# Weight additions and lower parts on VectorE, products with V in one run, and a planner with other durations: an attention and SoLU kernel on one core

## The chip, the cores and the metric

The kernel runs on one core of a Trainium2 chip. Its engines are TensorE (PE in the profile), VectorE (DVE), ScalarE (ACT), GpSimd (POOL) and SyncE (SP), which here only issues transfers. Each engine takes its instructions in the order in which the program has them. The metric is the device time of one execution in microseconds, lower being better.

## The reference

Causal attention by blocks of 64, for 8 batches of 8 heads with 576 tokens and 64 columns a head; then two projections with a SoLU and a normalisation between them, on 4608 tokens:

```
scores = scale * q @ k.T                       # masked to block_i >= block_j
attn   = softmax(scores)
x      = (attn @ v), heads side by side        # 4608 x 512
h      = x @ w_in                              # 512 x 1024
solu   = h * softmax(h)
ln     = (solu - mean) / sqrt(var + 1e-6) * g_ln
out    = ln @ w_out                            # 1024 x 512
```

The weights come as float64, q, k and v as float32.

## The kernel before

The work falls into three kinds, which are all described to a planner as operations with an engine, a duration, what they read and write, and a key.

- **Weights** (`prep`, lines 316 to 337): 16 chunks of 128x512 words of float64. A chunk is loaded into `ub` (two buffers), limited on DVE (L323), scaled (L326 on DVE, or L324 on ACT), shifted (L327) and given its sign (L328) on DVE; POOL adds the lower word as an integer (L329); chunks of `w_out` are scaled by `g_ln` (L331, L332). Then it is split into an exact pair: an upper part (L333 on ACT or L334 on DVE) and the lower part, the difference of the two (L335, on POOL). The intermediate values lie in `xt[2]` and `ob`.
- **Attention** (`attention`, lines 374 to 546), for 32 pairs of heads, four pairs to a batch. Queries and keys are loaded and transposed (L400); but for the first four pairs, they are split into upper and lower parts (L416 to L430). Scores are made in six groups of PSUM columns (L441, L445, L449), masked (L465), the maxima taken on DVE (L469), the exponentials on ACT (L473), the sums inverted on DVE (L480, L481), and the probabilities scaled on POOL (L488) or DVE (L489). TensorE transposes them (L499), ACT copies them out (L371), and TensorE multiplies them with V (L533): two heads side by side, each with 64 columns of the array, in float32. There are two such operations for a pair, one for the first 256 queries (`ph` 0, four products) and one for the rest (`ph` 1, ten products); each opens a single-bank PSUM tile of its own when it comes up. Results are copied to `xt` (three batches deep).
- **Projections** (`moe`, lines 549 to 643), for 36 tiles of 128 tokens: `x` is split (L564, L568), multiplied with `w_in` in two halves of 12 products (L589), then on DVE and ACT the maximum, the exponentials into `ub`, and the product with the sum (L595 to L598); POOL centres (L599), ACT squares (L601), POOL takes the root (L612, L613), TensorE transposes (L624), ACT and DVE split (L628, L629), TensorE multiplies with `w_out` (L637), and the result is scaled (L641) and stored (L643).

The order on every engine is worked out when the program is built, by `Schedule.run` (lines 97 to 171): a list schedule over the dependences. Whenever an engine is free, it takes, of the operations that are ready, the one with the smallest key that finds its PSUM tile free (two tiles of two banks, "D", and four of one bank, "S"). Keys come from `PARAMS`, one offset for each kind of operation, plus the number of the pair or of the tile. An operation may have alternatives on other engines, each with a penalty that is added to its key; an alternative whose penalty is 3 or more is not offered (L69). `START` and `LAT` hold the engines' first free times and the delays between engines. The instructions are then emitted in that order. On the chip, semaphores enforce the dependences; the planned times themselves enforce nothing.

Of the kernel before, what the change touches and what calls it, by code (L numbers as in the profile page):

```python
# [11 lines left out]
F32 = mybir.dt.float32  # L12
# [19 lines left out]
NPT = 2  # L32
START = {"PE": 0.0, "ACT": 2930.0, "DVE": 0.0, "POOL": 2500.0, "SP": 560.0}
PARAMS = {
# [6 lines left out]
    "a_sp32": -5.767, "a_lf": -3.555, "a_w": 15.208, "a_xh": 37.196, "a_xl": 48.757, "a_c": 6.341,  # L41
    "a_o": 13.796, "ns32": 4, "np": 32, "l0": -6.655, "a_cl": 5.076,
# [7 lines left out]
class Schedule:  # L50
    """Orders the operations of all engines: a list schedule over their dependences, with
    durations from shapes alone. PSUM slots (of one or two banks) are given out as it goes,
    and an operation that several engines can do goes to the one that is free for it first."""
# [43 lines left out]
    def run(self):  # L97
# [5 lines left out]
        engfree = {e: START[e] for e in engs}  # L103
        events = [(t, i, 0, None, None) for i, t in enumerate(sorted(START.values()))]
# [12 lines left out]
        while events:  # L117
            t = events[0][0]
            while events and events[0][0] <= t:
                _, _, kind, o, e = heapq.heappop(events)  # L120
                if kind == 1:
# [566 lines left out]
```

## Time and profile before

| what | value |
|---|---|
| timed runs | 816.08 us median of 3 (815.44 to 816.29) |
| span of the profiled execution | 814.3 us (no other time of that execution is given) |
| TensorE busy | 787.6 us, 97% |
| DVE, ACT, POOL busy | 60%, 68%, 38% |
| mean granted TensorE clock | 0.994 |

The span runs from the first to the last instruction. The timed runs hold 1.8 us more than the span at the median. A matmul's end is modelled, so where the exact cost of a group of matmuls matters, the step from its start to the start of what follows is the better measure. "L533" is line 533 of the kernel.

### The profile page before, as it was taken

Reading aid. Unit: us, or ns where it says so; the run is one execution under the profiler, and the core shown is the slowest. Engines: PE = TensorE matmul, PEld = TensorE weight load, DVE = VectorE, ACT = ScalarE, POOL = GpSimd, SP = SyncE. Lnnn points to the kernel's source line nnn. Section 1 sums busy time; section 2 is a strip of 40 time slices with the busy share of each in tenths; the row PEclk is TensorE's granted clock in tenths of the full one; section 3 lists DMA queues with packets and bytes.
Section 4 is the critical chain, followed back from the end, with each engine's and each line's share of the span. In section 5 each row is a group of like instructions: output and inputs, shape, how many; then the busy total and the mean of one; then the engine's idle time right before and its main releaser. Section 6 shows DMA issues by size and latency. Waiting matters only on the chain.

```text
span 814.3 us, 14121 instructions
## 1 busy us (share of the span) xinstructions
PE 787.6 (97%) x4711; PEld 635.9 (78%) x4711; DVE 492.3 (60%) x1200; ACT 557.0 (68%) x1441; POOL 308.6 (38%) x468
## 2 busy tenths in 40 slices
PE   6878899999999999999999999999999999999998
PEld 5545678888888888888888888888888888788886
DVE  5999986655665555566665555555666655333332
ACT  6778787686877777777787777777777777434332
POOL 3567772243443323333333323233333333132210
PEclk9999999999999999999999999999999999999999
DMA  7457534143443343333333333433343320000000
GB/s 210 117 146 181 140 83 105 49 102 82 109 101 92 88 101 101 93 95 96 94 90 79 83 94 87 101 101 96 92 101 88 95 63 29 14 27 26 14 27 39
DMA packets 132760, 71.84 MB, mean 88 GB/s; under 512 B 118864, under 2 KB 118864, under 8 KB 132688
## 3 DMA queue, kind: packets, MB, share of 16 engines
q1 hardware_dynamic: 131632, 70.68, 34.0%
q8 instruction: 37, 0.61, 0.3%
q10 hardware_dynamic: 1056, 0.26, 0.2%
q14 instruction: 35, 0.29, 0.1%
HBM read 36.70 MB, written 9.44 MB: 57 GB/s over the span
## 4 chain that ended last, share of the span: by engine, by line
PE 86%; DVE 9%; issue 2%; ACT 1%; POOL 1%; DMA 0%; SPq 0%; DVEq 0%; POOLq 0%
PE ps L637 24%; PE ps L589 23%; PE ps L533 10%; PE ps L499 9%; PE ps L449 8%; PE ps L624 5%; PE ps L400 3%; PE ps L445 3%; DVE nm L469 2%; DVE pb L489 1%; DVE xt L326 1%; DVE xt L328 1%; DVE xt L327 1%; PE ps L441 1%; DVE ks L420 1%
## 5 line engine op out<-in xcount | busy, mean ns | idle before, releaser
L488 POOL TENSOR_SCALAR pb<-pb,rz 128x512 f32<-128x512 f32 (+4 forms) x270 | 148.8, 571 | 179.0 <-DVE rz L481 164.1
L473 ACT ACTIVATE pb<-ps,nm 128x128 f32<-128x128 f32 (+4 forms) x288 | 155.7, 551 | 61.6 <-DVE nm L469 61.5
L469 DVE TENSOR_REDUCE nm<-ps 128x1 f32<-128x128 f32 (+4 forms) x288 | 133.0, 504 | 4.3 <-PE ps L445 1.2
L599 POOL TENSOR_SCALAR ub<-ub,ms 128x1024 f32<-128x1024 f32 x36 | 41.0, 1140 | 190.0 <-DVE ms L598 190.0
L499 PE MATMUL ps<-ident,pb 128*128 128x128 f32 x800 | 106.0, 275 | 7.1 <-ACT pb L473 3.3
L371 ACT ACTIVATE pt<-ps 128x512 f32<-128x512 f32 (+1 forms) x224 | 108.7, 553 | 4.9 <-PE ps L499 4.3
L499 PEld LDWEIGHTS ps<-ident,pb 128*128 128x128 f32 x800 | 92.6, 141 | 23.3 <-ACT pb L473 3.6
L533 PE MATMUL ps<-pt,vr 128*64 128x320 f32 (+4 forms) x896 | 101.3, 366 | 0.7 <-ACT pt L371 0.5
L533 PEld LDWEIGHTS ps<-pt,vr 128*64 128x64 f32 x896 | 58.8, 137 | 41.7 <-issue 5.5
L449 PE MATMUL ps<-ks,qs 128*128 128x384 f32 (+1 forms) x448 | 84.5, 328 | 1.7 <-DMA qs<-qs 1.2
L589 PE MATMUL ps<-wih,xh 128*128 128x512 f32 x288 | 82.2, 407 | 2.9 <-DVE qtl L428 2.9
L637 PE MATMUL ps<-woh,ch 128*128 128x512 f32 x288 | 83.6, 411 | 0.0
L629 DVE TENSOR_TENSOR cl<-ps,ch 128x512 fp32r<-128x512 f32 x72 | 49.3, 685 | 56.6 <-ACT ch L628 56.6
L589 PE MATMUL ps<-wil,xh 128*128 128x512 f32 x288 | 79.6, 399 | 0.0
L637 PE MATMUL ps<-wol,ch 128*128 128x512 f32 x288 | 79.0, 396 | 0.0
L637 PE MATMUL ps<-woh,cl 128*128 128x512 f32 x288 | 78.8, 395 | 0.0
L589 PE MATMUL ps<-wih,xl 128*128 128x512 f32 x288 | 78.2, 393 | 0.0
L449 PEld LDWEIGHTS ps<-ks,qs 128*128 128x128 f32 x448 | 68.6, 191 | 7.2 <-ACT xh L564 1.0
L641 ACT ACTIVATE ob<-ps,ms 128x512 f32<-128x512 f32 x36 | 24.7, 687 | 71.5 <-PE ps L637 66.6
L596 ACT ACTIVATE ub<-ps,ms 128x1024 f32<-128x1024 f32 x36 | 40.1, 1115 | 46.2 <-DVE ms L595 46.1
L589 PEld LDWEIGHTS ps<-wil,xh 128*128 128x128 f32 x288 | 54.9, 191 | 12.9
L637 PEld LDWEIGHTS ps<-woh,cl 128*128 128x128 f32 x288 | 54.1, 188 | 13.0
(79 smaller groups left out, 1238.6 us busy)
## 6 DMA issues: line engine op xcount, KB each, us to landing
qs<-qs SPq DMA_DIRECT2D x56, 288.0 KB, 4.1
out_dram<-ob SPq DMA_DIRECT2D x36, 256.0 KB, 2.0
qr<-in_q_dram SPq DMA_DIRECT2D x64, 128.0 KB, 3.0
vr<-in_v_dram SPq DMA_DIRECT2D x64, 128.0 KB, 2.5
ks<-k2h SPq DMA_DIRECT2D x56, 144.0 KB, 2.5
kr<-in_k_dram SPq DMA_DIRECT2D x62, 128.0 KB, 2.7
ub<-in_moe_w_in_dram SPq DMA_DIRECT2D x8, 512.0 KB, 3.6
ub<-in_moe_w_out_dram SPq DMA_DIRECT2D x8, 512.0 KB, 3.7
```

Of the source, the lines that this page charges most:

```text
L371: op("ACT", t_act(n_), lambda: ACT.activation(aps()[0], aps()[1], AF.Copy, scale=scale), r=r, w=w, key=key, ps=ps, alts=[("DVE", t_dve(n_) ...
L449: PE.matmul(t[:, off : off + wid[u]], qs[h][:, 640 * n_ + 128 * i_ : 640 * n_ + 128 * i_ + 128], ks[h][:, 0 : wid[u]], start=n_ == 0, stop ...
L469: op("DVE", t_dve(wid[u]), lambda sp=sp, off=off, u=u: DVE.tensor_reduce(out=nm_[u], in_=PS(sp)[:, off : off + wid[u]], axis=AX.X, op=ALU. ...
L473: op("ACT", t_act(wid[u], 186), lambda sp=sp, off=off, u=u, zg=zg, zc=zc: ACT.activation(pb[:, poff[u] : poff[u] + wid[u]], PS(sp)[:, off ...
L488: op("POOL", 0.836 * nn + 243, lambda b=b, nn=nn, zg=zg, zc=zc: POOL.tensor_scalar(out=pb[:, poff[b] : poff[b] + nn], in0=pb[:, poff[b] : ...
L499: PE.transpose(t[:, (s_ - c0) * P : (s_ - c0 + 1) * P], pb[:, poff[b] + j * P : poff[b] + (j + 1) * P], ident)
L533: PE.matmul(PS(av)[half[h], 64 * o_ : 64 * (o_ + n_)], vt[:, j, 64 * h : 64 * h + 64], pt_.rearrange("p s q -> p (s q)")[:, 128 * s_ + 64 ...
L589: PE.matmul(o_, a_[:, c, :], w_[:, c, s_], start=(si == 0 and c == 0), stop=(si == 2 and c == NKI - 1))
L599: op("POOL", 1097, lambda: POOL.tensor_scalar(out=u, in0=u, scalar1=m[:, 3:4], scalar2=1.0, op0=ALU.add, op1=ALU.mult), r=[uk, ("m3", i)], ...
L624: PE.transpose(t_[:, c * P : (c + 1) * P], u[:, (4 * hf + c) * P : (4 * hf + c + 1) * P], ident)
L629: op("DVE", t_dve(512), lambda cs=cs, cps=cps: DVE.tensor_tensor(out=cl[:, cs, :].rearrange("p c q -> p (c q)"), in0=PS(cps), in1=ch[:, cs ...
L637: PE.matmul(o_, a_[:, c, :], w_[:, c, :], start=(hf == 0 and si == 0 and c == 0), stop=(hf == 1 and si == 2 and c == 7))
```

## The change

It has four parts. The integer addition of the weights and their lower part become DVE operations of 602 ns each, with POOL as the alternative. The two operations that multiply with V become one, which opens both PSUM tiles at once. The planner gets other durations for products and float32 products, adds 130 ns where TensorE changes between products with V and all else (`mode`), and plans POOL's operations, and those DVE operations that are marked `port`, never at the same time. All keys, penalties and offsets in `PARAMS` are new.

```diff
+SWITCH = 130.0
-    "nd": 2, "ld": 50.439, "lv": 1.808, "q": -3.52, "qe": 1.142, "s": 6.097, "se": -34.711, "sr": -9.155,
-    "sp": -24.637, "pt": -53.902, "pe": -29.441, "av": -40.478, "ae": -54.031, "x": -19.096, "h0": 30.197,
-    "hs": 1.049, "h": 10.087, "he": 5.197, "c": 29.273, "sq": 24.027, "ct": -50.339, "ce": -26.902,
-    "o": 12.508, "oe": 52.668, "w0": 4.753, "w1": 3.56, "q32": -49.338, "qe32": 2.512, "s32": -30.884,
-    "se32": -21.58, "sr32": -9.773, "sp32": 10.661, "pt32": -1.589, "pe32": 9.069, "av32": -26.682,
-    "ae32": -42.402, "ld32": 8.508, "lv32": 16.251, "e0": 19.063, "e1": 23.219, "e2": 43.479, "a_sp": 40.963,
-    "a_sp32": -5.767, "a_lf": -3.555, "a_w": 15.208, "a_xh": 37.196, "a_xl": 48.757, "a_c": 6.341,
-    "a_o": 13.796, "ns32": 4, "np": 32, "l0": -6.655, "a_cl": 5.076,
+    "nd": 2, "ld": 51.667, "lv": -25.298, "q": 16.851, "qe": 21.577, "s": -46.724, "se": -35.56,
+    "sr": -64.883, "sp": 19.339, "pt": -9.35, "pe": -19.617, "av": -20.093, "ae": -61.172, "x": -18.296,
+    "h0": 5.994, "hs": 0.904, "h": 12.384, "he": -10.186, "c": 23.52, "sq": 33.665, "ct": -55.927,
+    "ce": -21.489, "o": 14.183, "oe": 21.926, "w0": 13.58, "w1": 5.806, "q32": -88.948, "qe32": 7.175,
+    "s32": -11.147, "se32": -18.711, "sr32": -21.226, "sp32": -7.207, "pt32": 34.929, "pe32": 32.662,
+    "av32": -29.049, "ae32": -107.21, "ld32": 4.757, "lv32": 133.636, "e0": 4.803, "e1": 13.081,
+    "e2": 16.285, "a_sp": 21.679, "a_sp32": -3.355, "a_lf": -4.456, "a_w": 9.152, "a_xh": 36.812,
+    "a_xl": 79.986, "a_c": -9.941, "a_o": -99.362, "ns32": 4, "np": 32, "l0": -17.25, "a_cl": 33.492,
+    "a_ai": 9.64,
...
-    def op(self, eng, dur, fn, r=(), w=(), key=0.0, opens=None, ps=None, tail=0.0, alts=()):
+    def op(self, eng, dur, fn, r=(), w=(), key=0.0, opens=None, ps=None, tail=0.0, alts=(), port=False, mode=0):
+        o.port, o.mode = port, mode
-        o.uses = ps if ps is not None else opens
+        o.opens = () if opens is None else opens if isinstance(opens, tuple) else (opens,)
+        o.uses = o.opens if ps is None else (ps,)
-        if o.uses is not None:
-            self.users[o.uses] = self.users.get(o.uses, 0) + 1
-            (w if eng == "PE" else r).append(("ps", o.uses))
+        for x in o.uses:
+            self.users[x] = self.users.get(x, 0) + 1
+            (w if eng == "PE" else r).append(("ps", x))
...
+        portfree, mode = 0.0, 0
...
-                    if o.uses is not None:
-                        left[o.uses] -= 1
-                        if left[o.uses] == 0:
-                            heapq.heappush(events, (t + LAT[o.eng]["PE"], n, 3, o, None))
+                    for x in o.uses:
+                        left[x] -= 1
+                        if left[x] == 0:
+                            heapq.heappush(events, (t + LAT[o.eng]["PE"], n, 3, x, None))
-                    free[self.kind[o.uses]].append(self.slot[o.uses])
+                    free[self.kind[o]].append(self.slot[o])
-                    if o.opens is not None:
-                        if not free[self.kind[o.opens]]:
+                    port = e == "POOL" or e == "DVE" and o.port
+                    if port and portfree > t:
+                        heapq.heappush(events, (portfree, n, 0, None, None))
+                        n += 1
+                        continue
+                    if o.opens:
+                        kinds = [self.kind[x] for x in o.opens]
+                        if any(len(free[k]) < kinds.count(k) for k in kinds):
-                    elif o.uses is not None:
-                        until = max([v for x, v in held[o.uses].items() if x != e], default=0.0)
+                    elif o.uses:
+                        until = max([v for x, v in held[o.uses[0]].items() if x != e], default=0.0)
...
-                if best.opens is not None:
-                    self.slot[best.opens] = free[self.kind[best.opens]].pop(0)
-                    held[best.opens] = {}
-                if best.uses is not None:
-                    held[best.uses][e] = t + best.dur + 128
+                if e == "PE" and best.mode != mode:
+                    best.dur += SWITCH
+                    mode = best.mode
+                if e == "POOL" or e == "DVE" and best.port:
+                    portfree = t + best.dur
+                for x in best.opens:
+                    self.slot[x] = free[self.kind[x]].pop(0)
+                    held[x] = {}
+                for x in best.uses:
+                    held[x][e] = t + best.dur + 128
...
-        return max(107.0, n / 2.4 + 2.5)
+        return max(109.0, 0.4453 * n + 3.5)
-        return max(224.0, n / 0.6 + 29) if fp32 else max(106.0, n / 2.4 + 53.0)
+        return max(214.0, n / 0.6) if fp32 else max(106.0, n / 2.4 + 53.0)
...
-        op("POOL", 1225, lambda: POOL.tensor_tensor(out=T1.bitcast(I32), in0=T1.bitcast(I32), in1=T3.bitcast(I32), op=ALU.add), r=[k1, k3], w=[k1], key=key)
...
+        op("DVE", 602, lambda: DVE.tensor_tensor(out=T1.bitcast(I32), in0=T1.bitcast(I32), in1=T3.bitcast(I32), op=ALU.add), r=[k1, k3], w=[k1], key=key, port=True,
+           alts=[("POOL", 1225, lambda: POOL.tensor_tensor(out=T1.bitcast(I32), in0=T1.bitcast(I32), in1=T3.bitcast(I32), op=ALU.add), K["a_ai"])])
...
-        op("POOL", 1225, lambda: POOL.tensor_tensor(out=lo, in0=T1, in1=hi.bitcast(F32), op=ALU.subtract), r=[k1, (name, "h")], w=[(name, "l")], key=key,
-           alts=[("DVE", 602, lambda: DVE.tensor_tensor(out=lo, in0=T1, in1=hi.bitcast(F32), op=ALU.subtract), K["a_w"])])
...
+        op("DVE", 602, lambda: DVE.tensor_tensor(out=lo, in0=T1, in1=hi.bitcast(F32), op=ALU.subtract), r=[k1, (name, "h")], w=[(name, "l")], key=key, port=True,
+           alts=[("POOL", 1225, lambda: POOL.tensor_tensor(out=lo, in0=T1, in1=hi.bitcast(F32), op=ALU.subtract), K["a_w"])])
...
-            av = newps("S")
-            js = range(5) if ph else range(2)
-            def avmm(av=av, js=js, ph=ph):
+        avs = [newps("S"), newps("S")]
+        def avmm():
+            for ph, js in ((0, range(2)), (1, range(5))):
-                            PS(av)[half[h], 64 * o_ : 64 * (o_ + n_)],
+                            PS(avs[ph])[half[h], 64 * o_ : 64 * (o_ + n_)],
-            sel = [c for c in ptc if (c[1] <= 6) == (ph == 0)]
-            ptk = [(x, p % NPT, c0) for x in ("pt", "pt2") for c0, _ in sel]
-            op("PE", 54 + sum(t_two(64 * mov(j, 0, ph)[2], True) for j in js), avmm, r=ptk + [f"vr{i}"], key=kk, opens=av)
+        ptk = [(x, p % NPT, c0) for x in ("pt", "pt2") for c0, _ in ptc]
+        op("PE", sum(t_two(64 * mov(j, 0, ph)[2], True) for ph, js in ((0, range(2)), (1, range(5))) for j in js), avmm, r=ptk + [f"vr{i}"], key=kk, opens=tuple(avs), mode=1)
...
+            av = avs[ph]
...
-            op("PE", 12 * 216, hmm, r=wk + [("xh", i), ("xl", i)], key=key + K["h"], opens=hps if hf == 0 else None, ps=hps)
+            op("PE", 12 * 231.5, hmm, r=wk + [("xh", i), ("xl", i)], key=key + K["h"], opens=hps if hf == 0 else None, ps=hps)
...
-            op("PE", 12 * 216, omm, r=wk + [("ch", hf), ("cl", hf), ("ch2", hf)], key=key + K["o"], opens=ops_ if hf == 0 else None, ps=ops_)
+            op("PE", 12 * 231.5, omm, r=wk + [("ch", hf), ("cl", hf), ("ch2", hf)], key=key + K["o"], opens=ops_ if hf == 0 else None, ps=ops_)
```

Lines that differ only by `port=True` are left out: the mark goes on L323, L326, L327, L328, the two alternatives L332 and L334, the scaling of probabilities (L488, L489), the splitting of `x` (L564, L568, and their DVE forms) and the centring (L599, L600). Penalties of 3 or more still keep an alternative out: with the new values that holds for POOL's integer addition (`a_ai`) and lower part (`a_w`), not for DVE's centring (`a_c`) and scaling of the output (`a_o`).

More of the change, by code (lines that the diff above doesn't have):

```diff
@@ L322, in prep @@
         op("ACT", 520, lambda: ACT.activation(T3.bitcast(I32), raw[:, :, 0], AF.Copy, scale=2.0**-29), r=[kr_], w=[k3], key=key)
-        op("DVE", 335, lambda: DVE.tensor_scalar(out=T2, in0=high, scalar1=TOP, scalar2=-TOP, op0=ALU.min, op1=ALU.max), r=[kr_], w=[k2], key=key)
+        op("DVE", 335, lambda: DVE.tensor_scalar(out=T2, in0=high, scalar1=TOP, scalar2=-TOP, op0=ALU.min, op1=ALU.max), r=[kr_], w=[k2], key=key, port=True)
         op("ACT", 520, lambda: ACT.activation(T2, T2, AF.Copy, scale=DOWN), r=[k2], w=[k2], key=key,
@@ L329, in prep @@
-        op("POOL", 1225, lambda: POOL.tensor_tensor(out=T1.bitcast(I32), in0=T1.bitcast(I32), in1=T3.bitcast(I32), op=ALU.add), r=[k1, k3], w=[k1], key=key)
+                 ("DVE", 335, lambda: DVE.tensor_scalar(out=T2, in0=T2, scalar1=DOWN, scalar2=None, op0=ALU.mult), K["a_lf"])], port=True)
+        op("DVE", 335, lambda: DVE.tensor_scalar(out=T1.bitcast(U32), in0=T2.bitcast(U32), scalar1=3, scalar2=0x7FFFFFF8, op0=ALU.logical_shift_left, op1=ALU.bitwise_and), r=[k2], w=[k1], key=key, port=True)
@@ new lines, in prep @@
+        op("DVE", 602, lambda: DVE.scalar_tensor_tensor(out=T1.bitcast(U32), in0=T2.bitcast(U32), scalar=0x80000000, in1=T1.bitcast(U32), op0=ALU.bitwise_and, op1=ALU.bitwise_or), r=[k1, k2], w=[k1], key=key, port=True)
+        op("DVE", 602, lambda: DVE.tensor_tensor(out=T1.bitcast(I32), in0=T1.bitcast(I32), in1=T3.bitcast(I32), op=ALU.add), r=[k1, k3], w=[k1], key=key, port=True,
+           alts=[("POOL", 1225, lambda: POOL.tensor_tensor(out=T1.bitcast(I32), in0=T1.bitcast(I32), in1=T3.bitcast(I32), op=ALU.add), K["a_ai"])])
@@ L330, in prep @@
         if gcol is not None:
             op("ACT", 613, lambda: ACT.activation(T1, T1, AF.Copy, scale=gcol), r=[k1, "gt"], w=[k1], key=key,
[L332 removed]
+               alts=[("DVE", 400, lambda: DVE.tensor_scalar(out=T1, in0=T1, scalar1=gcol, scalar2=None, op0=ALU.mult), K["a_lf"])], port=True)
         op("ACT", 520, lambda: ACT.activation(hi, T1, AF.Copy), r=[k1], w=[(name, "h")], key=key,
[L334 removed]
@@ L524, in attention @@
         ]
-        for ph in range(2):
-            av = newps("S")
-            js = range(5) if ph else range(2)
-            def avmm(av=av, js=js, ph=ph):
+        avs = [newps("S"), newps("S")]
+        def avmm():
+            for ph, js in ((0, range(2)), (1, range(5))):
                 for j in js:
@@ L576, in xlo2 @@
                 DVE.tensor_tensor(out=xl[i][:, :, c0:c1], in0=xt[x][:, :, a0:a1], in1=xh[i][:, :, c0:c1].bitcast(F32), op=ALU.subtract)
-        op("ACT", t_act(512, 42 + 93 * (len(segs) - 1)), xhi, r=xk, w=[("xh", i)], key=key + K["x"], alts=[("DVE", 335 + 65 * (len(segs) - 1), xhi2, K["a_xh"])])
-        op("POOL", 1225, xlo, r=xk + [("xh", i)], w=[("xl", i)], key=key + K["x"], alts=[("DVE", 602 + 65 * (len(segs) - 1), xlo2, K["a_xl"])])
+        op("ACT", t_act(512, 42 + 93 * (len(segs) - 1)), xhi, r=xk, w=[("xh", i)], key=key + K["x"], alts=[("DVE", 335 + 65 * (len(segs) - 1), xhi2, K["a_xh"])], port=True)
+        op("POOL", 1225, xlo, r=xk + [("xh", i)], w=[("xl", i)], key=key + K["x"], alts=[("DVE", 602 + 65 * (len(segs) - 1), xlo2, K["a_xl"])], port=True)
         hps = newps("D")
```

11 lines of the change are left out of this document (4 added, 7 removed).

## The prediction

> **What bounds the kernel now.** I read the page first, then the busy time by stretches, then TensorE's timeline where its stretches were not full, then the groups of the weight instructions. The page's busy time and its chain of waits name TensorE:
>
> ```profile
> PE 787.6 (97%) x4711; PEld 635.9 (78%) x4711; DVE 492.3 (60%) x1200; ACT 557.0 (68%) x1441; POOL 308.6 (38%) x468
> PE 86%; DVE 9%; issue 2%; ACT 1%; POOL 1%; DMA 0%; SPq 0%; DVEq 0%; POOLq 0%
> ```
>
> A share over the whole span hides that there are two kernels in it. By stretches (busy us of PE, PEld, DVE, ACT, POOL; then the granted clock):
>
> ```profile
> 5.10:20.00 14.90, 9.25 (x45) 6.57 (x44) 11.41 (x31) 10.80 (x31) 4.47 (x5) 1.00 0.83 230
> 20.00:40.00 20.00, 16.79 (x77) 11.51 (x77) 19.44 (x42) 14.55 (x39) 10.54 (x10) 0.92 0.47 123
> 40.00:60.00 20.00, 14.82 (x87) 9.39 (x88) 19.35 (x48) 15.89 (x51) 13.23 (x12) 1.00 0.48 129
> 60.00:80.00 20.00, 16.75 (x128) 11.79 (x128) 19.56 (x36) 17.08 (x43) 14.21 (x15) 0.95 0.72 184
> 80.00:95.40 15.40, 12.29 (x70) 8.85 (x66) 15.00 (x34) 11.87 (x35) 12.58 (x14) 0.94 0.47 131
> 95.40:108.00 12.60, 12.19 (x75) 9.28 (x75) 11.46 (x21) 8.84 (x23) 8.14 (x8) 0.88 0.48 116
> 108.00:804.00 696.00, 695.55 (x4195) 570.40 (x4195) 395.36 (x992) 474.67 (x1221) 242.47 (x390) 1.00 0.31 79
> 804.00:814.30 10.30, 6.46 (x30) 4.90 (x28) 0.69 (x1) 1.86 (x3) 0.00 (x0) 1.00 0.13 51
> ```
>
> From 108 us on TensorE idles for 0.45 us of 696, with DVE at 57% and ACT at 68%: there only less work for TensorE shortens the time. From 5.1 to 108 us it idles 5.65 + 3.21 + 5.18 + 3.25 + 3.11 + 0.41 = **20.8 us**, and from 20 to 95 us VectorE is 97% busy. That is the stage of the weights. The span is 814.3 us, the median of the timed runs 816.08; so 1.8 us lie outside the span, and the sum is made against 816.1.
>
> **Part 1, the products with V in one run.** L533 is entered twice for each pair. TensorE's timeline (start, length, instructions; the step to the next row's start is the true cost), with the first and last runs and, at 61.70, one of two places where two runs happen to stand together:
>
> ```profile
> 30.35 0.87 PE L533 MATMUL ps<-pt,vr 128*64 128x256 f32 x8
> ...
> 61.70 2.93 PE L533 MATMUL ps<-pt,vr 128*64 128x320 f32 x28 [0.49 <-ACT pt L371]
> 64.56 1.09 PE L499 MATMUL ps<-ident,pb 128*128 128x128 f32 x8
> ...
> 407.83 0.87 PE L533 MATMUL ps<-pt,vr 128*64 128x256 f32 x8
> 408.64 0.66 PE L624 MATMUL ps<-ident,ub 128*128 128x128 f32 x4
> 409.22 2.27 PE L533 MATMUL ps<-pt,vr 128*64 128x320 f32 x20
> 411.43 0.66 PE L624 MATMUL ps<-ident,ub 128*128 128x128 f32 x4
> 411.84 1.86 PE L449 MATMUL ps<-ks,qs 128*128 128x384 f32 x12
> ...
> 699.00 2.28 PE L533 MATMUL ps<-pt,vr 128*64 128x320 f32 x20
> ```
>
> Apart, the two runs take 408.64 - 407.83 = 0.81 and 411.43 - 409.22 = 2.21, together 3.02 us; as one, 64.56 - 61.70 = 2.86: 0.16 less. The four transposes between two runs take 409.22 - 408.64 = 0.58, those after the second only 411.84 - 411.43 = 0.41, and at the end of the kernel, away from any such run, 0.35:
>
> ```profile
> 801.04 0.60 PE L624 MATMUL ps<-ident,ub 128*128 128x128 f32 x4
> 801.39 1.17 PE L637 MATMUL ps<-woh,ch 128*128 128x512 f32 x4
> 802.39 1.10 PE L637 MATMUL ps<-wol,ch 128*128 128x512 f32 x4
> 803.33 1.10 PE L637 MATMUL ps<-woh,cl 128*128 128x512 f32 x4
> ```
>
> So leaving a run costs 0.41 - 0.35 = 0.06. Entering costs 0.58 - 0.41 = 0.17, of which some 0.07 is the transposes' own tail, which elsewhere falls on the next group (802.39 - 801.39 = 1.00 against 803.33 - 802.39 = 0.94): 0.10 net. A run spared is worth 0.16 + 0.06 + 0.10 = **0.32 us**. There are 62 runs in the trace; 32 pairs need 32, so 30 go: **-9.6 us**. Three of them lie before 108 us, where TensorE waits anyway; without these it is -8.6, and I take **-9.2**. The bounds: the new scheduler's charge of 0.13 a change is for the planner alone, but 60 changes at it would be 7.8; at most all 30 are worth 9.6. The Trainium skill ("TensorEngine Tiling (Array Packing)", Key Properties) says that changing the tiling mode drains TensorE; it gives no price, and none is needed.
>
> The one run opens two of the four single-bank PSUM tiles at once; see the second rival.
>
> **Part 2, 32 weight instructions from POOL to DVE.** An alternative with a penalty of 3 or more is not offered. The two penalties (a_ai 9.6, a_w 9.2) are over that, so POOL gets none of these additions and lower parts; "first" means "only". Groups of before (busy, mean ns):
>
> ```profile
> L329 POOL TENSOR_TENSOR xt<-xt,ob 128x512 int32<-128x512 int32 x16 | 21.4, 1338 | 19.0 <-DVE xt L328 19.0
> L335 POOL TENSOR_TENSOR wil<-xt,wih 128x512 fp32r<-128x512 f32 x8 | 11.3, 1416 | 7.6 <-ACT wih L333 4.4 <-DVE wih L334 3.2
> L335 POOL TENSOR_TENSOR wol<-xt,woh 128x512 fp32r<-128x512 f32 x8 | 10.6, 1321 | 2.7 <-DVE woh L334 1.7 <-ACT woh L333 1.0
> L326 DVE TENSOR_SCALAR xt<-xt 128x512 f32<-128x512 f32 x16 | 14.4, 918 | 0.1
> L328 DVE SCALAR_TENSOR_TENSOR xt<-xt 128x512 uint32<-128x512 uint32 x16 | 12.1, 758 | 0.1
> L489 DVE TENSOR_SCALAR pb<-pb,rz 128x256 f32<-128x256 f32 (+4 forms) x18 | 9.7, 589 | 0.0
> ```
>
> Off POOL go 43.3 us. No such addition runs on DVE before. The nearest row is L328, with the same size and two inputs; its shortest and median are 649 and 672 ns:
>
> ```profile
> L326 DVE TENSOR_SCALAR xt<-xt x16: 404/992/1503, 7.2 to 104.3; 128x512 f32<-128x512 f32 x16
> L328 DVE SCALAR_TENSOR_TENSOR xt<-xt x16: 649/672/1641, 9.8 to 107.1; 128x512 uint32<-128x512 uint32 x16
> ```
>
> I take 0.67: 32 x 0.67 = **+21.4 us on DVE** (20.8 by the shortest, 24.3 by the mean of 758). Against it stands what POOL costs DVE today. L326 needs 404 ns and takes 918 on average, (918 - 404) x 16 = 8.2 us lost; L328 loses (758 - 649) x 16 = 1.7. The Trainium skill ("SBUF — State Buffer", Who interferes with whom) has a rule that speaks against the change: a VectorE instruction with two SBUF inputs also waits for the port that it shares with GpSimd. L328's 1641 against 649 agrees. By it the moved instructions go on colliding with POOL's scalings, and the sum would lean to rival A.
>
> With POOL rid of 43 us most of those 9.9 us come back; I take 8. Of the 18 scalings of L489 (9.7 us) POOL, now freer, can take half: 5. Net on DVE: 21.4 - 8 - 5 = **+8 us** in a stage where it is full (bounds: 20.8 - 9.9 - 9.7 = +1, and +24.3 with nothing returned). So by load alone the startup gets longer.
>
> By order it gets shorter. Two of TensorE's waits stand here with DVE's queue ahead of them:
>
> ```profile
> 33.15 3.13 DVE L489 TENSOR_SCALAR pb<-pb,rz 128x128 f32<-128x128 f32 x4
> 36.88 1.84 DVE L326 TENSOR_SCALAR xt<-xt 128x512 f32<-128x512 f32 x2
> 38.64 0.75 DVE L469 TENSOR_REDUCE nm<-ps 128x1 f32<-128x576 f32 x1
> 42.25 1.13 PE L441 MATMUL ps<-kf,qf 128*128 128x512 f32 x2 [3.31 <-ACT pb L473]
> 95.36 2.04 PE L589 MATMUL ps<-wih,xh 128*128 128x512 f32 x4 [2.86 <-DVE qtl L428]
> ```
>
> The maximum at 38.64 came behind scalings and weight steps stretched by POOL, the exponentials behind it, TensorE behind them: 3.31 us. The first projection waited 2.86 us for a PSUM tile that DVE read late, and its first four products then took 2.04 instead of 1.1 us at a granted clock of 0.88. A plan that knows the shared port need not put such work there, and a weight chunk no longer hops to POOL and back twice. All of both is 3.31 + 2.86 + 0.94 = 7.1 us; of that and like waits I count 11 as within reach (half of 20.8) and 8 as lost by load: **-3 us** (from -12, when load costs nothing, to +8, when order gains nothing).
>
> What is late next: each tile's exponentials write ub, the buffer of the raw weights, so tile 0 cannot pass its softmax before the last chunks are read. The new keys put chunks 2 to 15 later (13.6 + 5.8n instead of 4.8 + 3.6n), behind all attention work on DVE. Loads of V for the first four pairs go behind the weight loads in SP's order (key 134 instead of 16). SP mostly waits for ub in that time, so I price this at nothing; if that cover is gone, the first run of products waits for a landing.
>
> **Part 3, the rest.** Durations (231.5 instead of 216 for a product of 512 columns), the charge and the port change the order alone. The centring (L599) may now go to DVE; after 108 us that is hidden under a full TensorE, and DVE at 57% has room for it. Priced at nothing.
>
> **Sum.** 816.1 - 9.2 - 3 = **803.9 us**.
>
> **The rivals.** *A: the startup pays.* The +8 us of DVE work all lands on the path and order returns nothing: 816.1 - 9.2 + 8 = 814.9. If the moved instructions are stretched as L328 is, (758 - 649) x 32 = 3.5 us of DVE's time come on top; half of that on the path would make it 816.6. For: DVE's 97%. Against: in those stretches TensorE's waits were also for ACT and POOL in turn.
>
> *B, the slower side: two PSUM tiles at once.* The run of products needs two free single-bank tiles of four; while one is free, a transpose or score group with any key takes it. If on average each of 32 runs holds TensorE until one more copy out of PSUM is over, the row for that copy gives its price:
>
> ```profile
> L371 ACT ACTIVATE pt<-ps 128x512 f32<-128x512 f32 (+1 forms) x224 | 108.7, 553 | 4.9 <-PE ps L499 4.3
> ```
>
> 32 x 0.553 = 17.7; 816.1 - 9.2 + 17.7 = 824.6. It decides from 0.3 us a pair on. For: only four such tiles. Against: TensorE idles 0.45 us of 696 today, so it has other work to take meanwhile.
>
> *C: the startup nearly heals.* With better order and no collisions -12: 794.9.
>
> *D: the change doesn't do what it says,* because a stall of B's kind gives back the 9 us: 816.
>
> **How the numbers follow.** Forecast (798 to 810) 0.58, A (810 to 815) 0.16, C (below 798) 0.12, B 0.09, D 0.05. 1.6 us, 0.2%, is what a measurement of this kernel can tell from no change. So faster 0.58 + 0.16 + 0.12 = 0.86, same 0.05, slower 0.09. The range reaches to A and C: 794 to 815.
>
> **What would show it.** L533 in 32 runs of 28, each 2.86 us; TensorE full after the startup. L329 and L335 gone from POOL, and on DVE near 0.67 us; L326 below 0.6. TensorE's idle time before 108 us near 18 us instead of 20.8. I am wrong if TensorE idles inside the long stretch ahead of L533, or if its first products of L589 come later than 95 us with more idle time ahead of them.

## The result and the profile after

The changed kernel takes **835.4 us** at the median (834.12 to 837.8) against 816.15 us of the kernel before in the same rounds: a ratio of 1.0239 [1.0222, 1.0256]. It is slower by 2.4%, where 803.9 was forecast and 815 was the upper end of the range. The profiled execution has a span of 833.0 us. Seventeen or eighteen lines were added above the attention code, so the line numbers have moved: L449 (score products) is now L467, L430 (the copy of the queries) L448, L499 L517, L533 L550, L589 L607, L624 L642, L637 L655.

The page's busy time, chain of waits and the group of the score products, of the changed kernel:

```profile
PE 789.5 (95%) x4711; PEld 640.5 (77%) x4711; DVE 498.1 (60%) x1257; ACT 554.4 (67%) x1444; POOL 238.6 (29%) x408
PE 68%; DVE 12%; ACT 9%; DMA 8%; issue 3%; SPq 0%; POOL 0%; ACTq 0%; POOLq 0%; DVEq 0%
PE ps L607 23%; PE ps L655 13%; PE ps L467 8%; PE ps L517 8%; DMA qs<-qs 6%; PE ps L550 5%; PE ps L463 3%; DVE ks L438 2%; PE ps L642 2%; PE ps L459 2%; DVE ub L615 2%; PE ps L418 2%; DVE qs L446 2%; ACT qs L445 1%; ACT pt L389 1%
L467 PE MATMUL ps<-ks,qs 128*128 128x384 f32 (+2 forms) x448 | 90.4, 331 | 20.7 <-DMA qs<-qs 13.8
```

TensorE's part of the chain has fallen from 86% to 68%, and transfers, at 0% before, now hold 8%. Of this, 6% is one transfer: `qs<-qs`, the copy that L448 makes of the split queries from one half of the partitions to the other. TensorE idled 20.7 us ahead of the score products, 13.8 of them put down to that copy. The name is that of the last releaser in the profile, and it can mislead: 24 of these waits, 19.5 us together, ended within 0.2 us after such a copy had landed, whatever the profile names. Two stand in the startup:

```profile
85.31 0.76 PE L467 MATMUL ps<-ks,qs 128*128 128x384 f32 x4 [2.21 <-DMA qs<-qs]
88.17 2.26 PE L467 MATMUL ps<-ks,qs 128*128 128x384 f32 x8 [2.10 <-ACT xh L582]
```

The second is put down to ACT, but the copy that was issued at 82.62 landed 5.46 us later, at 88.08. The same two kernels by stretches (busy us of PE, PEld, DVE, ACT, POOL, then the granted clock, the mean share of the DMA engines and GB/s; PEld is TensorE's weight loads), first the kernel before:

```profile
5.10:120.00 114.90, 94.00 (x537) 67.35 (x536) 107.29 (x233) 89.95 (x244) 73.78 (x75) 0.96 0.55 144
120.00:300.00 180.00, 179.64 (x1147) 147.14 (x1146) 107.64 (x278) 133.05 (x353) 65.35 (x107) 1.00 0.39 95
300.00:700.00 400.00, 400.00 (x2498) 328.96 (x2498) 238.06 (x605) 290.76 (x770) 142.88 (x236) 1.00 0.34 87
```

And after, with a row more for the startup up to 108 us:

```profile
5.10:108.00 102.90, 85.78 (x493) 62.84 (x492) 85.14 (x225) 88.33 (x241) 21.44 (x31) 0.90 0.59 153
...
5.10:120.00 114.90, 96.24 (x554) 71.56 (x554) 95.63 (x254) 98.63 (x268) 24.43 (x36) 0.91 0.58 150
120.00:300.00 180.00, 173.84 (x1082) 142.49 (x1079) 110.55 (x278) 124.59 (x328) 59.73 (x100) 1.00 0.34 83
300.00:700.00 400.00, 388.48 (x2409) 319.47 (x2408) 224.97 (x574) 272.39 (x718) 126.19 (x212) 1.00 0.34 85
```

The stretch that was full is no longer full: TensorE idles 6.2 us from 120 to 300 and 11.5 us from 300 to 700, where it idled 0.4 and 0.0, and it gets through 1082 + 2409 products there instead of 1147 + 2498. The startup is not where the time went: up to 120 us TensorE idles 18.7 us instead of 20.9, and it has issued 17 products more, though the granted clock is 0.91 instead of 0.96.

One place shows what happens again and again. TensorE's and SP's timeline of the changed kernel:

```profile
284.69 1.27 SPq L448 DMA_DIRECT2D qs<-qs  x2
...
287.03 0.60 PE L642 MATMUL ps<-ident,ub 128*128 128x128 f32 x4
...
289.19 1.97 PE L467 MATMUL ps<-ks,qs 128*128 128x384 f32 x12 [1.56 <-DMA qs<-qs]
```

The four transposes end by 287.63, and the scores start 4.50 us after the first copy was issued, when it has landed. In the kernel before the copy ahead of the scores at 411.84 was issued at 402.15, which is 9.7 us ahead:

```profile
402.15 1.38 SPq L430 DMA_DIRECT2D qs<-qs  x2
```

Over the pairs 4 to 31, the median from the issue of a pair's first copy to the pair's first score product is 10.0 us before and 3.8 us after. The next rows give the copy's own time from issue to landing, of the kernel before and of the changed one:

```profile
DMA to landing us min/median/max: 3.2/4.1/5.1
```

```profile
L448 SPq DMA_DIRECT2D qs<-qs x56: 461/513/1937, 63.7 to 721.2; - x56
...
DMA to landing us min/median/max: 3.0/3.6/7.0
```

The planner believes in 0.82 + 2.10 = 2.92 us (the copy's planned duration on SP and its `tail`), which is less than the shortest landing in either trace. Before, some six microseconds of slack beyond the landing covered the error. The new order leaves hardly any.

### The profile page after: what moved, and what is told of

It reads as the page before. It is cut to its first block, busy times and chain, and to the rows that moved or that the text cites. A ratio compares the mean times of both kernels' runs of the same rounds, so it can differ in the third digit from the quotient of the medians.

```text
span 833.0 us, 14113 instructions
## 1 busy us (share of the span) xinstructions
PE 789.5 (95%) x4711; PEld 640.5 (77%) x4711; DVE 498.1 (60%) x1257; ACT 554.4 (67%) x1444; POOL 238.6 (29%) x408
## 4 chain that ended last, share of the span: by engine, by line
PE 68%; DVE 12%; ACT 9%; DMA 8%; issue 3%; SPq 0%; POOL 0%; ACTq 0%; POOLq 0%; DVEq 0%
PE ps L607 23%; PE ps L655 13%; PE ps L467 8%; PE ps L517 8%; DMA qs<-qs 6%; PE ps L550 5%; PE ps L463 3%; DVE ks L438 2%; PE ps L642 2%; PE ps L459 2%; DVE ub L615 2%; PE ps L418 2%; DVE qs L446 2%; ACT qs L445 1%; ACT pt L389 1%
## 5 line engine op out<-in xcount | busy, mean ns | idle before, releaser
L506 POOL TENSOR_SCALAR pb<-pb,rz 128x384 f32<-128x384 f32 (+4 forms) x262 | 144.3, 569 | 281.1 <-DVE rz L499 163.3
L487 DVE TENSOR_REDUCE nm<-ps 128x1 f32<-128x128 f32 (+4 forms) x288 | 130.9, 498 | 1.6 <-PE ps L459 0.5
L517 PE MATMUL ps<-ident,pb 128*128 128x128 f32 x800 | 106.7, 279 | 9.9 <-DVE pb L507 2.1
L467 PE MATMUL ps<-ks,qs 128*128 128x384 f32 (+2 forms) x448 | 90.4, 331 | 20.7 <-DMA qs<-qs 13.8
L517 PEld LDWEIGHTS ps<-ident,pb 128*128 128x128 f32 x800 | 91.9, 143 | 21.9 <-ACT pb L491 3.2
L550 PE MATMUL ps<-pt,vr 128*64 128x320 f32 (+4 forms) x896 | 93.4, 360 | 0.9 <-ACT pb L491 0.9
L467 PEld LDWEIGHTS ps<-ks,qs 128*128 128x128 f32 x448 | 68.4, 192 | 29.1 <-ACT ch L646 5.4
L550 PEld LDWEIGHTS ps<-pt,vr 128*64 128x64 f32 x896 | 59.1, 137 | 40.1 <-ACT pb L491 2.8
L613 DVE TENSOR_REDUCE ms<-ps 128x1 f32<-128x1024 f32 x36 | 44.0, 1222 | 73.0 <-PE ps L607 73.0
L655 PE MATMUL ps<-woh,ch 128*128 128x512 f32 x288 | 83.1, 410 | 0.6 <-ACT ch L646 0.6
L607 PE MATMUL ps<-wih,xh 128*128 128x512 f32 x288 | 81.8, 406 | 0.0
L655 PE MATMUL ps<-wol,ch 128*128 128x512 f32 x288 | 78.9, 396 | 0.0
L607 PE MATMUL ps<-wil,xh 128*128 128x512 f32 x288 | 78.9, 396 | 0.0
L655 PE MATMUL ps<-woh,cl 128*128 128x512 f32 x288 | 78.6, 394 | 0.0
L607 PE MATMUL ps<-wih,xl 128*128 128x512 f32 x288 | 78.5, 394 | 0.0
L586 POOL TENSOR_TENSOR xl<-xt,xh 128x512 fp32r<-128x512 f32 (+1 forms) x40 | 47.0, 1182 | 98.1 <-PE ps L607 58.7
L483 DVE MEMSET ps<- 64x128 f32 (+1 forms) x160 | 22.6, 144 | 71.4 <-PE ps L467 64.5
L607 PEld LDWEIGHTS ps<-wil,xh 128*128 128x128 f32 x288 | 54.3, 188 | 12.8
L607 PEld LDWEIGHTS ps<-wih,xl 128*128 128x128 f32 x288 | 54.1, 188 | 13.0
```

What stands on the lines that cost most here:

```text
L467: PE.matmul(t[:, off : off + wid[u]], qs[h][:, 640 * n_ + 128 * i_ : 640 * n_ + 128 * i_ + 128], ks[h][:, 0 : wid[u]], start=n_ == 0, stop ...
L487: op("DVE", t_dve(wid[u]), lambda sp=sp, off=off, u=u: DVE.tensor_reduce(out=nm_[u], in_=PS(sp)[:, off : off + wid[u]], axis=AX.X, op=ALU. ...
L506: op("POOL", 0.836 * nn + 243, lambda b=b, nn=nn, zg=zg, zc=zc: POOL.tensor_scalar(out=pb[:, poff[b] : poff[b] + nn], in0=pb[:, poff[b] : ...
L517: PE.transpose(t[:, (s_ - c0) * P : (s_ - c0 + 1) * P], pb[:, poff[b] + j * P : poff[b] + (j + 1) * P], ident)
L550: PE.matmul(PS(avs[ph])[half[h], 64 * o_ : 64 * (o_ + n_)], vt[:, j, 64 * h : 64 * h + 64], pt_.rearrange("p s q -> p (s q)")[:, 128 * s_ ...
L586: POOL.tensor_tensor(out=xl[i][:, :, c0:c1], in0=xt[x][:, :, a0:a1], in1=xh[i][:, :, c0:c1].bitcast(F32), op=ALU.subtract)
```

## The experiments

Three theories were set against each other. **Theory 1**: the new keys order the work so that score products come just when the planner believes that the copy has landed, and TensorE stands until it really has. **Theory 2**: the single run of products with V costs more than it saves, because it holds two of four single-bank PSUM tiles (or because it starts later). **Theory 3**: the weights' additions on DVE cost the startup more than they return. Letters in the expectations are variants of these.

**The copy made short, order untouched.** In the changed kernel the copy moves 64 columns of 1152. For all pairs but the first four, the half of the query tile that the copy fills is then zero beyond these columns; that part of the computation is left out. Every planned duration stays, so the order on each engine stays too.

```diff
-  POOL.memset(qs[h][:, 576 - 64 * h : 640 - 64 * h].bitcast(F32), 0.0)
+  POOL.memset(qs[h].bitcast(F32), 0.0)
-  SP.dma_start(qs[h][oth].bitcast(F32), qs[h][own].bitcast(F32))
+  SP.dma_start(qs[h][oth, 0:64].bitcast(F32), qs[h][own, 0:64].bitcast(F32))
```

> The changed kernel with its order untouched; only the copy of the queries' parts from one half of the partitions to the other (L448) moves 64 of 1152 columns (the rest is zero from a memset at the start), so it lands sooner. The scores of pairs 4 to 31 are then computed from data that is partly zero. Theory 1 (late copies: the new order asks for the scores 2.92 us after the copy's issue, while the copy lands after 3.6 us, and TensorE stands ahead of L467): most of the 27 us of waits ahead of L467 go, 812 to 820 us. Theory 2 (the run with V holds two PSUM tiles) and theory 3 (the startup pays for the moved weight work): no change, 833 to 837 us.

Measured: **806.45 us** (805.96 to 807.76), 0.989 [0.9874, 0.9907] of the kernel before and 29 us below the changed kernel, which is more than theory 1 had asked for. (The page has 20.7 us of idle time ahead of L467, not the 27 that the expectation names.) The stretches, and the same place as above in this kernel's timeline:

```profile
5.10:120.00 114.90, 98.66 (x623) 73.06 (x622) 103.95 (x270) 106.40 (x289) 30.07 (x46) 0.97 0.56 144
120.00:300.00 180.00, 179.00 (x1098) 148.53 (x1097) 113.04 (x290) 126.47 (x335) 58.24 (x96) 1.00 0.25 63
300.00:700.00 400.00, 397.88 (x2479) 329.98 (x2477) 238.35 (x608) 280.23 (x742) 130.68 (x220) 1.00 0.26 64
```

```profile
272.32 1.14 SPq L448 DMA_DIRECT2D qs<-qs  x2
...
274.63 0.60 PE L642 MATMUL ps<-ident,ub 128*128 128x128 f32 x4
274.99 1.87 PE L467 MATMUL ps<-ks,qs 128*128 128x384 f32 x12
```

```profile
DMA to landing us min/median/max: 1.7/2.0/5.1
```

The copy lands in 2.0 us instead of 3.6, and the scores follow the transposes by 0.36 us instead of 2.16. From 120 to 700 us TensorE idles 3.1 us instead of 17.7. So the whole loss hangs on the size of this one transfer. The transfer of the keys (`ks<-k2h`) lands 2.5 us after issue at the median in both kernels, so it is not that the others got faster. The planner's 2.92 us lies above the short copy's median of 2.0 and below the long one's 3.6. By the Trainium skill ("DMA: Bandwidth & Descriptors", Anatomy of one DMA) a transfer costs a fixed 2 us or so and bytes over 436 GB/s, stated for another queue than SP's; an estimate from it is 2.0 us for 16 KB, which agrees with 2.0, and 2.7 for 288 KB, where the trace has 3.6 at the median and up to 7.0. The measurement decides.

The same edit in the kernel before (the same part left out):

> The same shortened copy in the kernel before; the scores of pairs 4 to 31 are computed from partly zero data. There the scores start about 10 us after the copy's issue. All theories: no change, 815 to 817 us. If it gains more than 3 us, theory 1's test says less than it seems to.

Measured: 816.54 us, 1.0009 [0.9998, 1.0019]. The copy costs nothing where 10 us lie between it and its reader, and the zeros in the data change nothing either.

**The weights alone.** The integer additions and the lower parts of the kernel before go to DVE, with no alternative; its keys and planner stay.

```diff
-  op("POOL", 1225, lambda: POOL.tensor_tensor(out=T1.bitcast(I32), ..., op=ALU.add), ...)
+  op("DVE", 602, lambda: DVE.tensor_tensor(out=T1.bitcast(I32), ..., op=ALU.add), ...)
-  op("POOL", 1225, lambda: POOL.tensor_tensor(out=lo, ..., op=ALU.subtract), ..., alts=[("DVE", 602, ..., K["a_w"])])
+  op("DVE", 602, lambda: DVE.tensor_tensor(out=lo, ..., op=ALU.subtract), ...)
```

> The kernel before with another part alone: the weights' integer additions and lower parts on VectorE; keys, durations and the two runs with V as before. Theory 3: the 8 us of net work on VectorE land on the path, 822 to 828 us. Theory 1: within 4 us of before, 812 to 820 us.

Measured: 817.09 us, 1.0013 [1.0004, 1.0023]. Theory 3 had asked for 822 or more and falls; under the old keys the move costs about 1.1 us (0.0013 x 816) and does not bring the 3 us that I had hoped for.

**The run of products alone.** In the kernel before, the two operations become one that opens both PSUM tiles.

```diff
-  for ph in range(2):
-      av = newps("S")
...
-      op("PE", 54 + ..., avmm, r=ptk + [f"vr{i}"], key=kk, opens=av)
+  avs = [newps("S"), newps("S")]
...
+  op("PE", 108 + ..., avmm, r=ptk + [f"vr{i}"], key=kk, opens=tuple(avs))
```

> The kernel before with one part of the change: the products with V in one run that opens two PSUM tiles; keys, durations and weights as before. Theory 1: the run is worth 30 x 0.32 us and the score products keep their slack, 805 to 809 us. Theory 2: TensorE waits ahead of L533 or for single-bank tiles, 818 us or more.

Measured: **824.65 us**, 1.0108 [1.0093, 1.0123]. I had counted on a gain here, and it is a loss of 8.8 us (0.0108 x 816). The stretches of this kernel:

```profile
5.10:120.00 114.90, 90.15 (x513) 64.04 (x513) 102.75 (x231) 86.65 (x235) 68.92 (x68) 0.96 0.51 137
120.00:300.00 180.00, 173.54 (x1085) 142.45 (x1084) 103.36 (x271) 127.68 (x345) 62.50 (x104) 0.98 0.38 92
300.00:700.00 400.00, 399.75 (x2522) 329.69 (x2521) 235.46 (x611) 290.25 (x776) 144.75 (x238) 1.00 0.36 90
```

From 300 to 700 us TensorE is all but full and gets through 24 products more than before. The first score products of pairs 14 and 30 give the length of a pair; their rows in the timelines of the kernel before and of this one:

```profile
300.00 0.59 PE L449 MATMUL ps<-ks,qs 128*128 128x384 f32 x2
...
657.87 0.42 PE L449 MATMUL ps<-ks,qs 128*128 128x384 f32 x1
```

```profile
309.43 0.42 PE L451 MATMUL ps<-ks,qs 128*128 128x384 f32 x1
...
664.83 0.42 PE L451 MATMUL ps<-ks,qs 128*128 128x384 f32 x1
```

A pair takes (657.87 - 300.00) / 16 = 22.37 us before and (664.83 - 309.43) / 16 = 22.21 here. Both stretches hold the same products, 16 pairs and 16 tiles. So in this order a spared run returns some **0.15 us, not 0.32**. The loss lies before 300 us: idle time grows from 20.9 to 24.8 and from 0.4 to 6.5 us. To place it further, the one run was made for pairs 8 to 31 only:

```diff
+  if p >= 8:
+      avs = [newps("S"), newps("S")]
...
+  else:
+      for ph in range(2):
+          av = newps("S")
...
```

> The kernel before with the products with V in one run for pairs 8 to 31 alone; the first eight pairs keep two runs, so the order of the startup stays. If the run alone lost time because it disturbed the startup: 24 pairs at 0.15 to 0.32 us less, 808 to 813 us. If the run itself costs (two PSUM tiles at once): 818 us or more.

Measured: 815.05 us, 0.9984 [0.9975, 0.9994], between the two times that had been named. So the first eight pairs cost (1.0108 - 0.9984) x 816 = 10.1 us, and the other 24 bring 1.3 us. Two more kernels take the run apart: in one, the two operations stay apart but both wait for all seven groups of probabilities; in the other they start when they did, but the first opens both tiles.

```diff
-  sel = [c for c in ptc if (c[1] <= 6) == (ph == 0)]
+  sel = ptc
```

> The kernel before, with two runs of products with V as it has them, but both wait for all seven groups of transposed probabilities, as one run has to. This tells apart why the one run alone (with the old keys) lost 8 us. Theory 2a (the loss is the later start): 821 us or more. Theory 2b (the loss is the hold on two PSUM tiles): 814 to 819 us.

Measured: 818.64 us, 1.003 [1.0019, 1.0041].

```diff
+  avs = [newps("S"), newps("S")]
...
-  op("PE", 54 + ..., avmm, ..., opens=av)
+  op("PE", 54 + ..., avmm, ..., opens=None if ph else tuple(avs), ps=av if ph else None)
```

> The kernel before, with two runs that start when they did, but the first opens the PSUM tiles of both at once. Theory 2b (the hold on two of four single-bank tiles): 821 us or more, with TensorE's waits in the first 300 us. Theory 2a: 814 to 819 us.

Measured: **846.83 us**, 1.0375 [1.0356, 1.0394]. The later start costs 2.4 us (0.003 x 816), the hold 30.6. Its stretches and TensorE's waits:

```profile
5.10:120.00 114.90, 89.47 (x486) 63.03 (x485) 103.34 (x217) 81.66 (x220) 65.51 (x60) 0.90 0.52 137
...
300.00:700.00 400.00, 387.45 (x2463) 317.38 (x2462) 228.08 (x599) 287.38 (x779) 142.27 (x237) 1.00 0.37 89
```

```profile
PE ps L451 <- ACT pb L475: 9.9, 9, 1.7
PE ps L451 <- DMA qs<-qs: 4.6, 4, 1.7
```

Two held tiles of four make TensorE idle 12.6 us from 300 to 700, ahead of scores (L451 here). But this hold is longer than that of a single run, since both tiles are taken at the first operation and the second may come much later. In the one run the hold costs nothing from 300 us on (full, above), so the price of 30.6 is an upper bound for the mechanism and not its price in the changed kernel.

**The keys alone.** The changed kernel with the keys, penalties and offsets of the kernel before (and the new penalty of the integer additions):

```diff
-  "nd": 2, "ld": 51.667, "lv": -25.298, "q": 16.851, ...
+  "nd": 2, "ld": 50.439, "lv": 1.808, "q": -3.52, ..., "a_ai": 9.64,
```

> The changed kernel with the keys, penalties and offsets of the kernel before (POOL's penalty for the integer addition as in the changed one); run with V in one, weights on VectorE, durations, charge and port as changed. Theory 1a (the new keys alone bring the score products up against the copy's landing): few waits ahead of L467, 804 to 816 us. Theory 1b (the planner's new durations and port do it, with any keys): 828 us or more, with the waits.

Measured: 822.0 us (819.52 to 825.67), 1.0075 [1.0045, 1.0104], between what the two variants had named. So the new keys are 13.4 us of the loss, net of what they gain, and the code with the old keys loses some 6 us as well. A copy now has 6.1 us at the median before its reader, and TensorE idles 0.7 us from 300 to 700 us. What is left lies early, as in the kernel with the run of products alone; the largest wait is for the same copy:

```profile
PE ps L466 <- DMA qs<-qs: 9.9, 6, 6.0
```

**The planner told of the landing.** First in the changed kernel with its keys:

```diff
-  op("SP", 410, lambda ...: SP.dma_start(ks[h][own].bitcast(F32), k2h[own].bitcast(F32)), ..., tail=2100)
+  op("SP", 410, lambda ...: SP.dma_start(ks[h][own].bitcast(F32), k2h[own].bitcast(F32)), ..., tail=2500)
-  op("SP", 820, lambda ...: SP.dma_start(qs[h][oth].bitcast(F32), qs[h][own].bitcast(F32)), ..., tail=2100)
+  op("SP", 820, lambda ...: SP.dma_start(qs[h][oth].bitcast(F32), qs[h][own].bitcast(F32)), ..., tail=3500)
```

> The changed kernel with one thing told otherwise to its planner: the two kinds of copies between halves of the partitions (L437, L448) land 0.4 and 1.4 us later than it believed, which is past the 3.6 us from issue to landing in the trace. The planner makes a new order of its own from that. Theory 1: the waits ahead of L467 go, 806 to 822 us (the new order may leave gaps elsewhere). If the waits are not due to the planner's belief: 830 us or more.

Measured: 825.78 us, 1.0113 [1.0097, 1.0129]: 9.6 us better than the changed kernel, though not the 13 to 29 expected. Waits that ended within 0.2 us after a copy's landing are down from 19.5 us to 5.9 (of which the profile names 1.7; the 3.3 that it puts down to DVE are among them). But the order that follows has gaps of its own in the startup, where TensorE idles 20.9 us up to 120 instead of 18.7:

```profile
PE ps L517 <- ACT pb L491: 4.3, 5, 2.3
PE ps L467 <- DVE xt L340: 3.3, 1, 3.3
...
PE ps L467 <- DMA qs<-qs: 1.7, 2, 1.0
```

Keys are fitted to the durations that they were chosen with, so the next kernel has tails of 2500 and 3300 and keys chosen for these, all else as in the changed kernel.

> The changed kernel with its planner told of the landings (0.4 and 1.2 us later than it believed) and keys chosen anew for that. Theory 1: TensorE full after the startup as in the kernel before, 803 to 816 us; the startup decides where in it. If what a planner does not know costs more than this (later landings apart, the port and clock in the startup), 817 us or more.

Measured: 812.14 us (809.15 to 813.16), 0.9946 [0.9925, 0.9966], within the range; but TensorE is not full after the startup, it idles 4.1 us from 120 to 300 and 2.0 from 300 to 700. The new penalties also offer POOL the integer additions again, and it does 5 of the 16.

**The copy on another engine.** GpSimd, or DVE as the alternative, copies the queries between the halves; no transfer is left to be late. First with the keys of the changed kernel:

```diff
-  op("SP", 820, lambda ...: SP.dma_start(qs[h][oth].bitcast(F32), qs[h][own].bitcast(F32)), ..., tail=2100)
+  op("POOL", 1270, lambda ...: POOL.tensor_copy(qs[h][oth], qs[h][own]), ..., port=True,
+     alts=[("DVE", 665, lambda ...: DVE.tensor_copy(qs[h][oth], qs[h][own]), K["a_qd"])])
```

> The changed kernel, keys untouched, with the copy L448 done by POOL or DVE (planned at 1.27 and 0.67 us) instead of a transfer of 3.6 us; nothing is left out. The planner orders anew. Theory 1: the score products wait for no transfer of the queries any more, 804 to 822 us. If the waits belong to the new keys and not to the late transfer, they appear ahead of the same products with POOL or DVE as the one waited for, and the time stays at 828 us or more.

Measured: 825.17 us, 1.0112 [1.0095, 1.0129], above the range that theory 1 had named. The scores now wait for the keys' transfer, which comes late in the same way, and other work:

```profile
PE ps L518 <- ACT pb L492: 5.6, 6, 2.4
PE ps L468 <- DMA ks<-k2h: 3.6, 4, 1.3
```

Then with the tail of L437 at 2500 and keys chosen for this:

> The copy L448 on POOL or DVE as in the run before this one's, L437's landing told 0.4 us later, and keys chosen anew for it. Theory 1: 801 to 814 us, with TensorE full after the startup.

Measured: **804.96 us** (804.36 to 805.96), 0.9865 [0.985, 0.988], the whole computation done; it beats the kernel before and the changed one. Not all of the change is in it: its keys have penalties below 3 for POOL's integer additions and lower parts, and POOL does 13 of the 32. Its stretches and the groups of the copy:

```profile
5.10:120.00 114.90, 97.48 (x605) 73.24 (x604) 100.40 (x239) 100.84 (x279) 66.64 (x79) 0.94 0.57 145
120.00:300.00 180.00, 178.88 (x1124) 147.47 (x1123) 120.52 (x300) 133.65 (x355) 83.51 (x121) 1.00 0.26 64
300.00:700.00 400.00, 400.00 (x2505) 330.19 (x2504) 239.88 (x603) 280.70 (x752) 166.44 (x248) 1.00 0.24 59
```

```profile
L446 POOL CAST qs<-qs 64x1152 fp32r<-64x1152 f32 x27 | 31.2, 1156 | 6.4 <-DVE qs L444 3.7 <-DVE z L497 1.1
L447 DVE CAST qs<-qs 64x1152 fp32r<-64x1152 f32 x29 | 24.5, 844 | 0.9
```

The long stretch is full again, and the copy takes 1.16 or 0.84 us on engines that are busy for 42% and 62% of the span, instead of 3.6 us at the median in flight.

The pair is shorter here, too. The stretches from pair 14 to pair 30 in the kernel before, in the one with the run of products alone, and in this one (time, then TensorE's busy time and products):

```profile
300.00:657.87 357.87, 357.87 (x2243) 1.00 0.37 92
309.42:664.83 355.41, 355.16 (x2243) 1.00 0.37 93
279.06:633.08 354.02, 354.02 (x2243) 1.00 0.27 66
```

With the same products a pair takes 354.02 / 16 = 22.13 us, 0.24 less than before. What of this is the one run, and what the order around it, was not taken apart.

## Why the prediction was wrong

**The step that failed is Part 3**: "Durations ... the charge and the port change the order alone. ... Priced at nothing", and the statement it rests on, that from 108 us on TensorE idles 0.45 us of 696 and so only less work for it shortens the time. That is true of the order it was read from. A TensorE that is full under one order need not be full under the next. In the old order 10.0 us lay between the copy and its reader; the changed code leaves 6.1 of them with the old keys and 3.8 with the new ones. The copy with its real length under the new order costs 29 us. I had the page in hand (4.1 us to landing) and the planner's 2.92 us in the code, and I compared neither with the other.

**Part 1 was too large too.** As foretold, the runs are fewer: 30 in the trace after (28 of 28 products and 2 of 56, where two pairs stand together) instead of 62. A run takes what I had read off:

```profile
351.54 2.92 PE L550 MATMUL ps<-pt,vr 128*64 128x256 f32 x28
```

In the trace its steps come to 2.86 us. But under the old keys a spared run returned 0.15 us in the steady pairs, and 1.3 us over the last 24 pairs together: that is no more than the 0.16 inside the run, and the 0.16 for entering and leaving was not seen. In the last kernel, with other keys, a pair is 0.24 us shorter. So the -9.2 should have been between -4.5 (30 x 0.15) and, if all of the 0.24 is the run's, -7.2 (30 x 0.24), before the startup takes its share.

**Part 2's sum came out near its size by other steps.** The weight instructions after:

```profile
L345 DVE SCALAR_TENSOR_TENSOR xt<-xt 128x512 uint32<-128x512 uint32 x16 | 11.3, 709 | 0.1
L346 DVE CUSTOM_DVE_ANT_0 xt<-xt,ob 128x1024 uint16<-128x1024 uint16 x16 | 11.1, 694 | 0.1
L353 DVE TENSOR_TENSOR wol<-xt,woh 128x512 fp32r<-128x512 f32 x8 | 5.4, 677 | 0.2 <-ACT woh L351 0.2
L353 DVE TENSOR_TENSOR wil<-xt,wih 128x512 fp32r<-128x512 f32 x8 | 5.4, 671 | 0.0
L343 DVE TENSOR_SCALAR xt<-xt 128x512 f32<-128x512 f32 x6 | 2.8, 473 | 0.1
```

The moved instructions take 0.67 to 0.69 us (0.67 forecast), the collisions are mostly gone (473 ns for the six scalings that stay on DVE, from 918 for the sixteen of before; 709 from 758 for the sign), and POOL's busy time falls by 70 us. But DVE is not more loaded in the startup: it is busy 85.1 of 102.9 us up to 108, 83%, where the rows of the prediction sum to 96.2. Ten of the sixteen scalings went to ACT, and the new keys carry the weights on until 142 us instead of 113. TensorE idles 17.1 us there (18 forecast), and the first projection comes at 92.5 instead of 95.4. The forecast price of the load, +8, has no counterpart. Since these edits alone, under the old keys, cost 1.1 us (0.0013 x 816) and did not bring 3, what the startup gained here came with the rest of the change, the new keys most likely; that was not tried by itself.

**Rival B had the sign and not the place.** It named the two PSUM tiles and gave 824.6, and the run alone measured 824.65; this agreement is an accident of size, as the loss there is 10.1 us in the first eight pairs and none in the later 24, where B spread it over all 32. In the changed kernel the idle time lies ahead of L467, for a transfer that no rival named. My own test, idle time "ahead of L533", looked at the wrong group, and the first half of it, "TensorE full after the startup", failed.

**What the total hid.** With the copy short, 806.45 is within 3 us of 803.9. That must not be read as the terms being right: under the old keys the run alone cost 8.8 us and the weights alone 1.1, where -9.2 and -3 were forecast, so the agreement is in part luck. The pages tell where the 10 us lie: TensorE idles 26.0 us with the short copy and 26.7 before, so what fell is its busy time, from 787.6 to 777.5. How much of this is the one run and how much the order that the new keys and the planner's charge make, the very step that I had priced at zero, was not measured.

**The ledger** of the 29 us between the changed kernel and the one with the short copy: the spans are 833.0 and 803.5, and of the 29.5 us idle time is 43.5 - 26.0 = 17.5. The 19.5 us of waits that ended with a copy's landing are all gone, and other waits grew by 2.0. The mean granted clock of 0.987 against 0.996 makes 833.0 x 0.013 - 803.5 x 0.004 = 10.8 - 3.2 = 7.6 us, by estimate, of products at a lower clock, nearly all before 120 us (0.91 against 0.97 there). The largest piece stands right behind the two waits of the startup that are shown above:

```profile
87.10:93.90 6.80, 5.72 (x20) 5.27 (x21) 2.94 (x11) 3.30 (x13) 2.42 (x2) 0.50 0.37 107
```

With the short copy the clock is 1.00 in that part, and the first projection comes at 84.97 us instead of 92.52. That the waits lower the clock is not shown. The other 4.4 us stand as busy time, whose ends are modelled, and I have not placed them.

**What stays open**: which operation in the first eight pairs pays for the one run in the old order. The runs show only that a later start by itself costs some 2.4 us, and that holding two tiles can cost more than the rest. What the one run costs or brings in the changed kernel itself was not measured: no run has the new keys and two runs.

## What to carry to other kernels

An order made by a planner is only as good as the landing times it believes: compare each planned transfer with the trace's time to landing, and ask how much time lies between a transfer and its reader, because that slack hides the error until another order spends it. An engine that is full under one order need not be full under the next, so new keys should not be priced at nothing. To see whether a transfer is late, make it short and leave the order alone; if the time falls, either tell the planner and choose the keys again, or move the copy to an idle engine.

## What the runs showed of the hardware

- A copy of 64 partitions x 1152 floats (288 KB) from one half of SBUF's partitions to the other lands 3.6 to 4.1 us after issue at the median, and up to 7.0; one of 16 KB in 2.0. DVE does the large one in 0.84 us and GpSimd in 1.16, partitions changed, which I had not expected to be so much less.
- The int32 addition on DVE appears in the trace as `CUSTOM_DVE_ANT_0` over 1024 uint16 elements, at 694 ns, within 4% of a float32 subtraction of 512 elements (671 to 677 ns).
- A landing can be late by far more than its median: 7.0 us against 3.6 in the changed kernel (issued at 78.2 us), 5.1 against 2.0 with the short copy (at 76.8), in the startup, where the DMA engines are at a mean share of 0.58 and 0.56 up to 120 us. Whether that share makes them late was not tried.
